# A gated mix of linear attention and a spatial MLP: w_phi laid out block-diagonally by eight small loads in place of TensorE, with the bias row, the attention weights and wo loaded in other pieces

## The chip, the cores and the metric

The kernel runs on one core of a Trainium2 chip. The metric is the device time of one execution in microseconds. Before the change the median of five runs is 208.5 us (208.04 to 208.77). One execution was also profiled; all durations and starts below are from it, in microseconds from the first instruction.

The engines are named as in the profile: PE is TensorE (PEld its weight loads), DVE is VectorE, ACT is ScalarE, POOL is GpSimd, SP is SyncE. SPq and ACTq are the instruction rows of SyncE and ScalarE, from which loads and transposes are issued.

## The reference

The input x has 2048 rows of 512. Three things are computed and mixed:

```
g  = sigmoid(sum(x * gate_w))                       # one value for each row
A: q, k, v = x @ wqkv, 32 heads of 16
   pq = q @ w_phi[h], pk = k @ w_phi[h]             # one 16x16 matrix for each head
   phi = concat(softmax(p), softmax(-p))            # 32 features, for q and for k
   kv = phi_k^T v ; z = sum over s of phi_k
   a  = (phi_q @ kv / (phi_q . z + 1e-6)) @ wo
B: z = gelu(x @ w_in) ; z1, z2 = halves of 688      # z2 is layer-normalized
   gg = w_sp @ z2 + b_sp                            # mixes the 2048 rows
   b  = (z1 * gg) @ w_out
out = g * a + (1 - g) * b
```

## The kernel before

The rows are worked on in 16 tiles of 128 (NT = 16). All is bf16, with sums in fp32.

**First stage, to about 45 us.** For each tile TensorE multiplies x (held transposed in xT) by the two halves of w_in (z_one, L195); ScalarE applies gelu into z2all and z1all; VectorE takes mean and variance (L211 to L214), and z2_norm (L276) normalizes four tiles at a time. The order on TensorE and ScalarE is written out by hand (manual_schedule): in the loop over c (four tiles each), z2 tiles, then z1 tiles. The order on SyncE, VectorE and GpSimd is made by the compiler, which plans with its own costs.

Inside this stage w_phi is folded into the q and k weights, so that pq and pk come from one product. For this w_phi must lie block-diagonally: tile wphi has 128 partitions and four blocks (kc) of 128 columns, and in block kc the eight heads 8*kc to 8*kc+7 lie as 16x16 squares on the diagonal, zero elsewhere. Before the change this layout is made in three steps. One load puts w_phi into 16 partitions of wphiE (L140). wphi_fold (L302), called after c == 1, multiplies wphiE by a 0/1 matrix eexp, which repeats the 16 rows in all eight groups of 16 partitions (four matmuls, L305), and VectorE multiplies the result by a block mask mask_bd while copying it into wphi (L310). eexp and mask_bd are made by GpSimd (L151 to L161). Then fold(qk) (L324) multiplies the transposed weights wqkT by wphi in 32x32 pieces; fold(1), for k, is done at c == 2 and fold(0), for q, at c == 3.

The bias b_sp is needed as a column for each tile. A row tile brow, of which 16 partitions are loaded by a GpSimd DMA (L118), is transposed by one matmul with the identity in b_T (L299), called after z2_tile(3), and copied to bT by VectorE (L300).

The small PSUM tiles of this stage (x transposes, gate, b_T, wphi_fold, half of a fold) take turns in two buffers, pq0 and pq1 (pq_tile).

**SyncE's queue** issues, in this order: x tiles and w_in, six transposes of x (L135, L137), w_phi (L140), the transpose of the q and k weights into wqkT in one piece (L141), the v weights wv in one load (L142), and w_sp transposed in four pieces (L147). Later it issues transposes of eq, o and ucat and, after row tile 7 of the second stage, wo and w_out into slabs of wspT that are no longer read (load_out_weights, L450 to L457).

**Second stage, from 45 us.** For each tile: k and q features (L372, L376), v (L412), the kv sums (L428), and half a tile of w_sp @ z2 (L463), whose result VectorE joins with bT and z1all into ucat (L468). Then, with kv complete, attention (L476), and the output products with wo (L500) and w_out (L502, L505), scaled and stored (L516).

The lines that the change touches are 72 to 75 (tiles), 116 to 118, 140 to 145, 151 to 164, 302 to 312, 340, 354 and 450.

Of the kernel before, what the change touches and what calls it, by code (L numbers as in the profile page):

```python
# [8 lines left out]
ALU = mybir.AluOpType  # L9
AX = mybir.AxisListType  # L10
FP32 = mybir.dt.float32
BF16 = mybir.dt.bfloat16
I32 = mybir.dt.int32

P = 128
S = 2048
D = 512
H = 32
DH = 16
# [3 lines left out]
NT = S // P  # L23
NDT = D // P
# [11 lines left out]
def kernel(  # L36
# [14 lines left out]
    nc = tc.nc  # L51
# [6 lines left out]
    early = early_cm.__enter__()  # L58
# [6 lines left out]
    wv_sb = kvw.tile([P, NDT, D], BF16, name="wv_sb")  # L65
# [3 lines left out]
    z2all = pers.tile([P, NT, FH], BF16, name="z2all")  # L69
    z1all = pers.tile([P, NT, FH], BF16, name="z1all")  # L70
    wqkT = early.tile([P, 8, D], BF16, name="wqkT")
    wphiE = early.tile([P, H, DH], BF16, name="wphiE")
    eexp = early.tile([P, P], BF16, name="eexp")
    wphi = early.tile([P, NDT, P], BF16, name="wphi")
    mask_bd = early.tile([P, P], BF16, name="mask_bd")
    mask64 = pers.tile([P, NG, DH], BF16, name="mask64")
    mask4 = pers.tile([P, NG], BF16, name="mask4")
    kvz = pers.tile([P, 8, AW], BF16, name="kvz")
# [17 lines left out]
    brow = early.tile([P, P], BF16, name="brow")  # L96
# [10 lines left out]
        out=ramp[:, 0, :], data0=ones32[:, :], data1=zeros[:, :], initial=0.0,  # L107
# [4 lines left out]
    for q in range(4):  # L112
        qs = slice(32 * q, 32 * q + 32)
        nc.vector.tensor_tensor(
            out=ident[qs, qs], in0=ramp[qs, 0, :], in1=ramp[qs, 1, :], op=ALU.is_equal)
    nc.gpsimd.memset(brow[:], 0.0)
    nc.gpsimd.memset(wphiE[:], 0.0)
    nc.gpsimd.dma_start(out=brow[0:NT, :], in_=B_b_sp.rearrange("(t p) -> t p", p=P))  # L118
    def load_z2w(eng, dt):
        eng.dma_start(out=w_z2[:, dt, 0:FH], in_=w_in_v[:, dt, FH:F])  # L120

# [8 lines left out]
        out=xs[:, 2:4, :], in_=x2[2 * P:4 * P, :].rearrange("(i p) d -> p i d", p=P))  # L130
    for h in range(2):
        nc.sync.dma_start(
            out=w_z1[:, 2 * h:2 * h + 2, :], in_=w_in_v[:, 2 * h:2 * h + 2, 0:FH])
    for i in range(4, 8):
        nc.sync.dma_start_transpose(out=xT[:, :, i * P:(i + 1) * P], in_=x2[i * P:(i + 1) * P, :])  # L135
    for q in range(2, NCH):
        nc.sync.dma_start_transpose(  # L137
            out=xT[:, :, q * CH:(q + 1) * CH], in_=x2[q * CH:(q + 1) * CH, :]
        )
    nc.sync.dma_start(out=wphiE[0:DH, :, :], in_=A_w_phi.rearrange("h e f -> e h f"))  # L140
    nc.sync.dma_start_transpose(out=wqkT[:, :, :], in_=A_wqkv[:, 0:2 * D])  # L141
    nc.sync.dma_start(  # L142
        out=wv_sb[:, :, :],
        in_=A_wqkv[:, 2 * D:3 * D].rearrange("(dt p) n -> p dt n", p=P),
    )
    for q in range(NCH):
        nc.sync.dma_start_transpose(  # L147
            out=wspT[:, :, q * CH:(q + 1) * CH], in_=B_w_sp[q * CH:(q + 1) * CH, :]
        )
    nc.gpsimd.memset(mhalf[:], -0.5)  # L150
    nc.gpsimd.memset(eexp[:], 0.0)  # L151
    nc.gpsimd.affine_select(
        out=eexp[:, :], in_=eexp[:, :], pattern=[[0, 8], [-1, 16]],
        compare_op=ALU.not_equal, fill=1.0, base=0, channel_multiplier=1,
    )
    nc.gpsimd.memset(mask_bd[:], 1.0)
    nc.gpsimd.affine_select(
        out=mask_bd[:], in_=mask_bd[:], pattern=[[-16, 8], [0, 16]],
        compare_op=ALU.is_ge, fill=0.0, base=0, channel_multiplier=1,
    )  # L160
    nc.gpsimd.affine_select(  # L161
        out=mask_bd[:], in_=mask_bd[:], pattern=[[16, 8], [0, 16]],
        compare_op=ALU.is_ge, fill=0.0, base=15, channel_multiplier=-1,
    )
    nc.gpsimd.memset(mask4[:], 1.0)
    nc.gpsimd.affine_select(
        out=mask4[:], in_=mask4[:], pattern=[[-32, NG]],
        compare_op=ALU.is_ge, fill=0.0, base=0, channel_multiplier=1,
    )
    nc.gpsimd.affine_select(  # L170
        out=mask4[:], in_=mask4[:], pattern=[[32, NG]],
        compare_op=ALU.is_ge, fill=0.0, base=31, channel_multiplier=-1,
    )
    nc.gpsimd.tensor_copy(
        out=mask64[:, :, :], in_=mask4[:, :, None].to_broadcast([P, NG, DH]))
# [7 lines left out]
    def next_turn(kind, n):  # L183
        turn[kind] += 1
        return f"{kind}{(turn[kind] - 1) % n}"
# [4 lines left out]
    def pq_tile(shape, dtype=FP32):  # L190
        return psF.tile(shape, dtype, name="pq", tag=next_turn("pq", 2))
# [24 lines left out]
    def z2_tile(tt):  # L216
        z2_out(tt, z_mm(tt, w_z2, FH + 1))
# [44 lines left out]
    def z1_tile(tt):  # L262
        zp = z_mm(tt, w_z1, FH)
        nc.scalar.activation(  # L264
            out=z1all[:, tt, :].rearrange("p (j n) -> p j n", j=2), in_=zp[:, :, 0:HF],
            func=AF.Gelu_apprx_tanh,
        )

    def z2_norm(ts):
        sl = slice(ts[0], ts[-1] + 1)  # L270
        nc.gpsimd.tensor_scalar(
            out=veps[:, sl], in0=mv[:, sl, 1], scalar1=1e-5, scalar2=None, op0=ALU.add
        )
        nc.gpsimd.tensor_tensor(out=rstd[:, sl], in0=veps[:, sl], in1=mhalf[:, sl], op=ALU.pow)
        for tt in ts:
            nc.vector.tensor_scalar(  # L276
                out=z2all[:, tt, :], in0=z2all[:, tt, :],
                scalar1=mv[:, tt, 0:1], scalar2=rstd[:, tt:tt + 1],
                op0=ALU.subtract, op1=ALU.mult,
            )  # L280
# [16 lines left out]
    def b_T():  # L297
        bt = pq_tile([P, NT])
        nc.tensor.matmul(bt[:, :], lhsT=brow[:, :], rhs=ident[:, 0:NT], start=True, stop=True)  # L299
        nc.vector.tensor_copy(out=bT[:, :], in_=bt[:, :])  # L300

    def wphi_fold():  # L302
        wps = pq_tile([P, NDT, P])
        for kc in range(NDT):
            nc.tensor.matmul(  # L305
                wps[:, kc, :], lhsT=eexp[:, :],
                rhs=wphiE[:, kc * 8:(kc + 1) * 8, :].rearrange("e h f -> e (h f)"),
                start=True, stop=True,
            )
        nc.vector.tensor_tensor(  # L310
            out=wphi[:, :, :], in0=wps[:, :, :],
            in1=mask_bd[:, None, :].to_broadcast([P, NDT, P]), op=ALU.mult,
        )

    def fold(qk):
        dst = (wq_p if qk == 0 else wk_p)[:].rearrange("p dt n -> p (dt n)").rearrange(
            "p (m r f) -> p r m f", r=4, f=32)
        pair = zp_tile()
        banks = [pair[:, 0, :], pair[:, 1, :], pq_tile([P, CH])[:, :], pq_tile([P, CH])[:, :]]
        for m in range(NDT * NDT):  # L320
            dt, kc = divmod(m, NDT)
            for r in range(4):
                rows = slice(32 * r, 32 * r + 32)
                nc.tensor.matmul(  # L324
                    banks[r][:, m * 32:(m + 1) * 32],
                    lhsT=wqkT[rows, qk * 4 + kc, dt * P:(dt + 1) * P],
                    rhs=wphi[rows, kc, rows], start=True, stop=True,
                )

        def take(out, in_):  # L330
            nc.scalar.copy(out=out, in_=in_.rearrange("p (m f) -> p m f", f=32))

        nc.scalar.copy(out=dst[:, 0:2], in_=pair[:, :, :].rearrange("p r (m f) -> p r m f", f=32))
        return [lambda: take(dst[:, 2], banks[2]), lambda: take(dst[:, 3], banks[3])]

    with tc.manual_schedule(engines={mybir.EngineType.PE, mybir.EngineType.Activation}):
        z2_first_two()
        z2_tile(2)
        z2_tile(3)
        b_T()  # L340
        for c in range(NCH):
            ts = list(range(c * 4, c * 4 + 4))
            for tt in ts:
                if c > 0:
                    z2_tile(tt)
                if c >= 2 and tt % 4 == 1:
                    later = fold(3 - c)
            for tt in ts:
                z1_tile(tt)
                if c >= 2 and tt % 2 == 0:  # L350
                    later.pop(0)()
            z2_norm(ts)
            if c == 1:
                wphi_fold()

    psA_cm.__exit__(None, None, None)
    psF_cm.__exit__(None, None, None)
# [87 lines left out]
    def load_out_weights():  # L445
        slabs = wspT[:, :, 0:D]
        w_main = [slabs[:, 0:5, :], slabs[:, 5:10, :]]
        w_rem, wo_t = slabs[:, 10, :], slabs[:, 11:11 + NDT, :]
        nc.gpsimd.memset(w_rem, 0.0)
        nc.sync.dma_start(out=wo_t, in_=A_wo.rearrange("(g p) n -> p g n", p=P))  # L450
        for i in range(2):
            nc.sync.dma_start(
                out=w_main[i],
                in_=B_w_out[i * REM:i * REM + 5 * P, :].rearrange("(ft p) n -> p ft n", p=P),
            )
        nc.sync.dma_start(out=w_rem[0:REM, :], in_=B_w_out[5 * P:FH, :])
        nc.sync.dma_start(out=w_rem[P - REM:P, :], in_=B_w_out[0:REM, :])  # L457
        return w_main, w_rem, wo_t
# [95 lines left out]
    with tc.manual_schedule(engines={mybir.EngineType.PE, mybir.EngineType.Activation}):  # L554
# [3 lines left out]
        for tt in range(NT):  # L558
# [7 lines left out]
            if tt == 7:  # L566
                w_main, w_rem, wo_t = load_out_weights()
# [51 lines left out]
```

The softmax here doesn't subtract the row's maximum and nothing guards it: scores larger than these inputs give would overflow.

## Time and profile before

| what | value |
|---|---|
| median of five runs | 208.5 us (208.04 to 208.77) |
| the profiled execution | 208.5 us |
| its span, first to last instruction | 206.8 us |
| granted TensorE clock | 0.999 |
| TensorE busy | 202.8 us, 98% of the span |
| VectorE / ScalarE / GpSimd busy | 129.0 / 77.0 / 46.5 us |
| L305, expansion of w_phi, TensorE | 4 matmuls of 128 columns |
| L310, mask multiply, VectorE | 0.69 us |
| L299, bias transpose, TensorE | 1 matmul of 16 columns |
| L140, w_phi load | 1.49 us to issue, 4.5 us to landing |
| L141, wqkT transpose | 4.57 us to issue, 6.7 us to landing |
| L118, bias load on GpSimd | 0.75 us to issue, 4.2 us to landing |

The page has six parts: busy time by engine; the span in 40 equal slices with the busy share in tenths; the transfer queues; the chain of work that ended last, which is followed back from the last instruction to what released each step; the costliest groups of instructions; and the issues of loads with their time to landing. A row of the timeline has the start, the length, the engine, the line, the operation, what it writes and reads, and how many like instructions are merged in it. For a load issue (SPq, ACTq) the length is that of the issue alone; the data land later. Matmuls of one row overlap in their last part, so their cost is read from the distance between starts, or from the chain.

### The profile page before, as it was taken

Reading aid. Unit: us, or ns where it says so; the run is one execution under the profiler, and the core shown is the slowest. Engines: PE = TensorE matmul, PEld = TensorE weight load, DVE = VectorE, ACT = ScalarE, POOL = GpSimd, SP = SyncE. Lnnn points to the kernel's source line nnn. Section 1 sums busy time; section 2 is a strip of 40 time slices with the busy share of each in tenths; the row PEclk is TensorE's granted clock in tenths of the full one; section 3 lists DMA queues with packets and bytes.
Section 4 is the critical chain, followed back from the end, with each engine's and each line's share of the span. In section 5 each row is a group of like instructions: output and inputs, shape, how many; then the busy total and the mean of one; then the engine's idle time right before and its main releaser. Section 6 shows DMA issues by size and latency. Waiting matters only on the chain.

```text
span 206.8 us, 3967 instructions
## 1 busy us (share of the span) xinstructions
PE 202.8 (98%) x1552; PEld 121.2 (59%) x1552; DVE 129.0 (62%) x278; ACT 77.0 (37%) x124; POOL 46.5 (22%) x78
## 2 busy tenths in 40 slices
PE   8999999999999999999999999999999999999994
PEld 4666666665666555556565666555455555665642
DVE  2477766656977776979797778555466553633330
ACT  3666668786322233333323032222261126002322
POOL 7020202020532327244242422222204220200000
PEclk9999999999999999999999999999999999999999
DMA  5999999999932025950413226756656467653442
GB/s 179 270 158 235 251 290 212 239 272 258 219 78 40 3 38 114 344 81 19 89 34 58 51 41 125 141 108 62 116 150 85 83 112 181 62 104 68 128 89 78
DMA packets 88971, 27.22 MB, mean 132 GB/s; under 512 B 82968, under 2 KB 88952, under 8 KB 88952
## 3 DMA queue, kind: packets, MB, share of 16 engines
q1 hardware_dynamic: 86176, 24.37, 60.5%
q10 hardware_dynamic: 2744, 2.60, 3.8%
q8 instruction: 12, 0.20, 0.4%
q14 instruction: 7, 0.06, 0.1%
q0 software_dynamic: 32, 0.00, 0.0%
HBM read 4.41 MB, written 2.10 MB: 31 GB/s over the span
## 4 chain that ended last, share of the span: by engine, by line
PE 96%; DMA 2%; SPq 0%; DVE 0%; issue 0%
PE mm L463 36%; PE zp L195 18%; PE mm L372 14%; PE mm L502 8%; PE mm L500 7%; PE mm L412 7%; DMA w_z<-in_B_w_in_dram 2%; PE at L476 2%; PE kvacc L428 2%; PE mm L505 1%; PE zp L324 0%; PE pq L284 0%; SPq L124 0%; SPq L122 0%; PE pq L324 0%; DVE ob L512 0%
## 5 line engine op out<-in xcount | busy, mean ns | idle before, releaser
L463 PE MATMUL mm<-z2all,wspT 128*128 128x344 bf16 x512 | 79.9, 309 | 0.0
L463 PEld LDWEIGHTS <-wspT 128*128 128x128 bf16 x512 | 49.0, 98 | 25.7 <-issue 0.4
L195 PE MATMUL zp<-w_z,xT 128*128 128x344 bf16 (+1 forms) x256 | 39.1, 310 | 0.1
L376 ACT ACTIVATE eq<-mm 128x512 bf16<-128x512 f32 x32 | 17.4, 594 | 51.3 <-POOL eq L389 21.5
L380 DVE TENSOR_REDUCE zs<-eq 128x64 f32<-128x1024 bf16 x16 | 19.5, 1220 | 20.3 <-ACT eq L376 20.3
L195 PEld LDWEIGHTS <-xT 128*128 128x128 bf16 x256 | 24.6, 98 | 12.0 <-issue 0.2
L468 DVE SCALAR_TENSOR_TENSOR ucat<-mm,bT,z1all 128x344 bf16<-128x344 f32 x32 | 17.4, 544 | 21.9 <-PE mm L463 21.9
L389 POOL TENSOR_TENSOR eq<-eq,ratio 128x512 bf16<-128x512 bf16 x16 | 16.9, 1056 | 50.2 <-DVE ratio L388 41.7
L376 ACT ACTIVATE ek<-mm 128x512 bf16<-128x512 f32 x32 | 17.3, 600 | 27.2 <-PE mm L372 27.2
L516 ACT ACTIVATE ob<-mm,g_inv 128x512 bf16<-128x512 f32 (+1 forms) x16 | 10.9, 681 | 32.8 <-PE mm L505 28.3
L380 DVE TENSOR_REDUCE zs<-ek 128x64 f32<-128x1024 bf16 x16 | 19.3, 1209 | 2.8 <-ACT ek L376 2.8
L502 PE MATMUL mm<-wspT,uT 128*128 128x512 bf16 (+2 forms) x85 | 20.1, 366 | 0.0
L372 PEld LDWEIGHTS <-xT 128*128 128x128 bf16 x128 | 12.2, 98 | 13.0 <-PE mm L505 0.8
L389 POOL TENSOR_TENSOR ek<-ek,ratio 128x512 bf16<-128x512 bf16 x16 | 16.9, 1057 | 2.0 <-DVE ratio L388 1.2
L500 PE MATMUL mm<-wspT,oT 128*128 128x512 bf16 (+2 forms) x68 | 16.6, 366 | 0.0
L372 PE MATMUL mm<-wq_p,xT 128*128 128x512 bf16 x64 | 16.4, 379 | 0.0
L412 PE MATMUL mm<-wv_sb,xT 128*128 128x512 bf16 x64 | 16.4, 379 | 0.0
L372 PE MATMUL mm<-wk_p,xT 128*128 128x512 bf16 x64 | 16.4, 379 | 0.0
L213 DVE BATCH_NORM_STATS2 bn<-z2all 128x6 f32<-128x344 bf16 x32 | 14.9, 502 | 0.0
L210 ACT ACTIVATE z2all<-zp 128x688 bf16<-128x688 f32 x16 | 11.8, 744 | 6.7 <-PE zp L195 6.3
L264 ACT ACTIVATE z1all<-zp 128x688 bf16<-128x688 f32 x16 | 11.9, 744 | 5.1 <-PE zp L195 5.1
L502 PEld LDWEIGHTS <-uT 128*128 128x128 bf16 x85 | 8.2, 98 | 9.2
(80 smaller groups left out, 147.5 us busy)
## 6 DMA issues: line engine op xcount, KB each, us to landing
out_dram<-ob ACTq DMA_DIRECT2D x15, 128.0 KB, 1.8
wspT<-in_B_w_out_dram SPq DMA_DIRECT2D x2, 640.0 KB, 4.9
w_z<-in_B_w_in_dram SPq DMA_DIRECT2D x2, 344.0 KB, 4.8
w_z<-in_B_w_in_dram ACTq DMA_DIRECT2D x3, 172.0 KB, 3.5
wv_sb<-in_A_wqkv_dram SPq DMA_DIRECT2D x1, 512.0 KB, 4.5
wspT<-in_A_wo_dram SPq DMA_DIRECT2D x1, 512.0 KB, 4.7
xs<-in_A_x_dram SPq DMA_DIRECT2D x2, 128.0 KB, 3.1
xs<-in_A_x_dram SPq DMA_DIRECT2D x1, 256.0 KB, 5.0
```

Source lines behind the costliest of these rows:

```text
L195: nc.tensor.matmul(zp[:, j, 0:n], lhsT=xT[:, dt, tt * P:(tt + 1) * P], rhs=wt[:, dt, j * HF:j * HF + n], start=(dt == 0), stop=(dt == NDT ...
L213: nc.vector.bn_stats(out=bn6[:, tt, j, :], in_=z2v[:, j, :])
L264: nc.scalar.activation(out=z1all[:, tt, :].rearrange("p (j n) -> p j n", j=2), in_=zp[:, :, 0:HF], func=AF.Gelu_apprx_tanh,)
L372: nc.tensor.matmul(ps[:, :], lhsT=xT[:, dt, tt * P:(tt + 1) * P], rhs=w[:, dt, :], start=(dt == 0), stop=(dt == NDT - 1))
L376: nc.scalar.activation(out=e[:, :, a, :], in_=ps[:, :].rearrange("p (h f) -> p h f", f=DH), func=AF.Exp, scale=1.0 - 2.0 * a)
L380: nc.vector.tensor_reduce(out=z[:].rearrange("p h a -> p (h a)"), in_=e[:].rearrange("p h a f -> p (h a) f"), axis=AX.X, op=ALU.add,)
L389: nc.gpsimd.tensor_tensor(out=e[:, :, 1, :], in0=e[:, :, 1, :], in1=ratio[:, :, None].to_broadcast([P, H, DH]), op=ALU.mult)
L412: nc.tensor.matmul(v_ps[:, :], lhsT=xT[:, dt, tt * P:(tt + 1) * P], rhs=wv_sb[:, dt, :], start=(dt == 0), stop=(dt == NDT - 1))
L463: nc.tensor.matmul(gp[:, 0:HF], lhsT=wspT[:, st, tt * P:(tt + 1) * P], rhs=z2all[:, st, j * HF:(j + 1) * HF], start=(st == 0), stop=(st == ...
L468: nc.vector.scalar_tensor_tensor(out=ucat[tt % NU][:, c0 + j * HF:c0 + (j + 1) * HF], in0=gp[:, 0:HF], scalar=bT[:, tt:tt + 1], in1=z1all[ ...
L500: nc.tensor.matmul(acc, lhsT=oT[:, g, :], rhs=wo_t[:, g, c0:c1], start=(g == 0), stop=False)
L502: nc.tensor.matmul(acc, lhsT=uT[:, i + ft, :], rhs=w_main[i][:, ft, c0:c1], start=False, stop=False)
```

## The change

The layout of wphi is made by loads: GpSimd clears wphi, and eight SyncE loads, one for each position u in the group of eight heads, put the 16x16 squares of heads u, u+8, u+16 and u+24 into 16 partitions of wphi. wphiE, eexp, mask_bd, wphi_fold and its mask multiply are gone. The bias row is loaded by SyncE, after the transposes of x, and b_T is called where wphi_fold was. The transpose into wqkT is in two pieces, the k weights first; the v weights and wo are loaded in two pieces each.

```diff
-    wphiE = early.tile([P, H, DH], BF16, name="wphiE")
-    eexp = early.tile([P, P], BF16, name="eexp")
     wphi = early.tile([P, NDT, P], BF16, name="wphi")
-    mask_bd = early.tile([P, P], BF16, name="mask_bd")
...
     nc.gpsimd.memset(brow[:], 0.0)
-    nc.gpsimd.memset(wphiE[:], 0.0)
-    nc.gpsimd.dma_start(out=brow[0:NT, :], in_=B_b_sp.rearrange("(t p) -> t p", p=P))
+    nc.gpsimd.memset(wphi[:], 0.0)
...
-    nc.sync.dma_start(out=wphiE[0:DH, :, :], in_=A_w_phi.rearrange("h e f -> e h f"))
-    nc.sync.dma_start_transpose(out=wqkT[:, :, :], in_=A_wqkv[:, 0:2 * D])
-    nc.sync.dma_start(
-        out=wv_sb[:, :, :],
-        in_=A_wqkv[:, 2 * D:3 * D].rearrange("(dt p) n -> p dt n", p=P),
-    )
+    nc.sync.dma_start(out=brow[0:NT, :], in_=B_b_sp.rearrange("(t p) -> t p", p=P))
+    for qk in (1, 0):
+        nc.sync.dma_start_transpose(
+            out=wqkT[:, qk * NDT:(qk + 1) * NDT, :], in_=A_wqkv[:, qk * D:(qk + 1) * D])
+    heads = A_w_phi.rearrange("(kc u) e f -> u e kc f", u=8)
+    for u in range(8):
+        us = slice(u * DH, (u + 1) * DH)
+        nc.sync.dma_start(out=wphi[us, :, us], in_=heads[u])
+    for h in range(2):
+        nc.sync.dma_start(
+            out=wv_sb[:, 2 * h:2 * h + 2, :],
+            in_=A_wqkv[h * 2 * P:(h + 1) * 2 * P, 2 * D:3 * D].rearrange("(dt p) n -> p dt n", p=P),
+        )
...
-    nc.gpsimd.memset(eexp[:], 0.0)
-    nc.gpsimd.affine_select(
...
-    nc.gpsimd.memset(mask_bd[:], 1.0)
-    nc.gpsimd.affine_select(
...
-    def wphi_fold():
...
         z2_tile(2)
         z2_tile(3)
-        b_T()
...
             if c == 1:
-                wphi_fold()
+                b_T()
...
-        nc.sync.dma_start(out=wo_t, in_=A_wo.rearrange("(g p) n -> p g n", p=P))
+        for h in range(2):
+            gs = slice(2 * h, 2 * h + 2)
+            nc.sync.dma_start(
+                out=wo_t[:, gs, :],
+                in_=A_wo[h * 2 * P:(h + 1) * 2 * P, :].rearrange("(g p) n -> p g n", p=P))
```

More of the change, by code (lines that the diff above doesn't have):

```diff
@@ L150 @@
     nc.gpsimd.memset(mhalf[:], -0.5)
-    nc.gpsimd.memset(eexp[:], 0.0)
-    nc.gpsimd.affine_select(
-        out=eexp[:, :], in_=eexp[:, :], pattern=[[0, 8], [-1, 16]],
-        compare_op=ALU.not_equal, fill=1.0, base=0, channel_multiplier=1,
-    )
-    nc.gpsimd.memset(mask_bd[:], 1.0)
-    nc.gpsimd.affine_select(
[L158 to L164, printed above, removed]
     nc.gpsimd.memset(mask4[:], 1.0)
@@ L300, in b_T @@
         nc.vector.tensor_copy(out=bT[:, :], in_=bt[:, :])
-    def wphi_fold():
[L303 to L313, printed above, removed]
     def fold(qk):
```

## The prediction

> **What bounds the kernel now.** I read the page's busy shares and slices first, then the chain of work that ended last, then that chain in order of time over the first 30 us.
>
> ```profile
> span 206.8 us, 3967 instructions
> PE 202.8 (98%) x1552; PEld 121.2 (59%) x1552; DVE 129.0 (62%) x278; ACT 77.0 (37%) x124; POOL 46.5 (22%) x78
> PE   8999999999999999999999999999999999999994
> PEclk9999999999999999999999999999999999999999
> DMA  5999999999932025950413226756656467653442
> PE 96%; DMA 2%; SPq 0%; DVE 0%; issue 0%
> ```
>
> TensorE is busy in every slice at full clock and is 96% of the chain. So a microsecond counts only if it is taken off TensorE's own row of instructions, or if TensorE is made to wait. The DMA line shows the second thing that matters: the transfers are saturated from 5 to 57 us (ten nines, slices of 5.2 us), and all the moved loads but that of wo lie in there.
>
> ```profile
> 1.74 4.48 DMA w_z<-in_B_w_in_dram
> 6.22 0.04 issue
> 6.26 1.33 PE zp L195 x8
> ...
> 8.62 2.34 PE zp L195 x16
> 10.96 0.01 PE pq L299
> 10.97 14.03 PE zp L195 x96
> 25.00 0.22 PE pq L305 x4
> 25.23 2.34 PE zp L195 x16
> 27.57 0.12 PE zp L324 x2
> ```
>
> Columns: start, length, what. From 6.26 us the chain is TensorE without a gap. The w_phi expansion (L305) stands in it with 0.22 us, the bias transpose (L299) with 0.01 us. 96 matmuls take 14.03 us, so 146 ns each.
>
> **The change, part by part.**
>
> *Expansion removed.* Four matmuls (L305) at 0.22 us in the chain go: **-0.22 us**. The VectorE mask multiply (L310, 0.69 us at 25.35) goes too, but VectorE then idles 1.17 us before its next work at 27.21: nothing. On GpSimd the bias DMA (0.75), eexp (0.23 + 0.37) and mask_bd (0.23 + 0.36 + 0.35) go, 2.29 us; all lie before 4.6 us, and GpSimd's next work, at 13.38, follows 8.79 us of idle: nothing. The memset of wphi replaces one of the same size (0.53 us).
>
> *Bias transpose moved* from 10.80 to where the expansion was. The chain's 0.01 us leaves one place and comes in at the other: zero (0.03 at most, from the starts of the neighbouring matmuls). Its VectorE copy (0.16) comes after the four normalizations that end at 25.44, into the gap before 27.21. It takes the expansion's place in the ring of two pq buffers and frees it at about 25.6, before the fold at 27.3. The row must be there by 24.8: issued at 14.1, it lands by 18.6 even at the 4.5 us that the w_phi load needed in that place.
>
> *Software queue emptied.* Over the first 10 us its 32 packets take 0.3% of the 16 transfer engines, 0.03 us of each. The chain there is the L120 load that ends at 6.22: between 0 and -0.2 us, the second being TensorE's gap before 6.26. I take **-0.03 us**, the row's own share.
>
> *The SyncE queue, 14 to 24 us.* This is the part that could cost something.
>
> ```profile
> 4.03 0.89 SPq L132 DMA_DIRECT2D w_z<-in_B_w_in_dram  x2
> 4.97 5.20 SPq L135 DMA_TRANSPOSE xT<-in_A_x_dram  x4
> 10.22 3.77 SPq L137 DMA_TRANSPOSE xT<-in_A_x_dram  x2
> 14.11 1.49 SPq L140 DMA_DIRECT2D wphiE<-in_A_w_phi_dram  x1
> 15.64 4.57 SPq L141 DMA_TRANSPOSE wqkT<-in_A_wqkv_dram  x1
> 20.26 0.58 SPq L142 DMA_DIRECT2D wv_sb<-in_A_wqkv_dram  x1
> 20.89 33.97 SPq L147 DMA_TRANSPOSE wspT<-in_B_w_sp_dram  x4
> ```
>
> New order: bias row from 14.11 (0.42, as the L122 to L129 loads take 0.41 to 0.44), two wqkT halves of 4.57 / 2 = 2.29 each, so the eight w_phi loads start at about 19.2. Each writes 16 partitions, 64 runs of 32 bytes. No row has this form. The bounds of one issue are 0.37 (the smallest SyncE load, L450 or the last store) and 1.49 (the whole w_phi load, 512 such runs). I take 0.47, an ordinary issue with its gap; an eighth of the runs stands nearer to it. Eight make 3.8, so the last would issue at about 22.5.
>
> One wait may come in. L132 at 4.03 is the ninth load issue of the program on the SyncE and ScalarE queues; it goes to a fresh tile and still waits 1.4 us, until the first load (0.81 + 3.1) has landed. I read this as eight completion semaphores used in turn. Counting on, the bias row is the 17th issue, the wqkT halves are 18 and 19, the w_phi loads 20 to 27. So the last w_phi load waits for the second half of wqkT. Undivided, wqkT landed 15.64 + 6.7 = 22.3. The transfers show 290 GB/s while it moves and about 1.5 us at 113 to 185 GB/s for w_phi's runs ahead of it (17.0 to 18.5). These 1.5 us move behind it, while between two parts of w_sp there is a dip of about 1 us, which the split may add: 21.8. That is before 22.5 and binds nothing. Landing takes 1.5 us (last store) to 4.5 (the old w_phi load, behind a transpose): I take 2.5, so w_phi is complete at 22.5 + 2.5 = **25.0**, and 27.0 at the longest. The fold needs it at 27.49 - 0.22 = **27.27**. Cost zero, cover 0.3 to 3.3 us.
>
> The partition-disjoint pair L456 and L457 (83.76 and 84.47, landing in 4.9) shows that such loads into one tile don't wait for each other.
>
> Behind it in the queue: the two wv loads, then w_sp, at about 23.9 in place of 20.89, 3.0 later. wv is read first at 47.0 and would land by about 28.4. The first part of w_sp, 12.0 to landing, comes at about 36 and is read first at 47.7: 11.7 us of cover, and the second part is read only at 84.0. The first uT transpose (56.29) goes 1 to 2 us later, and is read at 129.9. wo in two loads adds one issue of 0.37 to 0.57 at 81 us, ahead of uT, w_out and eqT transposes; wo is read at 129.0, the eqT at 117 and later. All nothing.
>
> *A rule against the change.* The rows: three loads issue at 0.81, 1.27 and 1.74 on SyncE and land 3.1 to 4.5 later, so latencies overlap. The Trainium skill, "DMA: Bandwidth & Descriptors", Rules for kernel authors, says to coalesce many small transfers, as one under 64 KB is mostly overhead, and its section on the anatomy of one DMA gives about 2.0 us of fixed cost. An estimate by that page with the eight one after the other is 16 us, complete at 35 and a stall of 8 us: 216. The rows speak against such a serial sum.
>
> **Sum.** The profiled execution took 208.5 us, 1.7 more than its span, and equals the median of the five runs (208.04 to 208.77). 208.5 - 0.22 - 0.03 = 208.25, span 206.55. That is 0.12%, less than the 0.2% (0.42 us) that a measurement of this kernel can tell from no change.
>
> **The rivals.**
>
> *More than the matmuls goes (faster).* For it: the bias load is the only use of the software queue, and 1.7 us lie outside the span, which the trace doesn't resolve; the start is bound by a load. Against it: its 32 packets are 0.3%. With the 0.2 us before 6.26 and another 0.15 of the 1.7 us: 208.5 - 0.22 - 0.2 - 0.15 = 207.9; bounds 207.5 and 208.08.
>
> *w_phi comes late (slower).* TensorE works in order, so the fold at L324 holds everything. It decides when the last load issues after 27.27 - 2.5 = 24.8, that is from (24.8 - 19.2) / 8 = 0.70 us an issue on. For it: one old issue took 1.49. At that price the last issue ends at 19.2 + 11.9 = 31.1 and lands by 32.6: a stall of 5.3, 213.6. Against it: all other plain issues lie at 0.34 to 0.66, and the old one went out just behind two transposes. A mild case, 1 us of stall, gives 209.25.
>
> *Another order on VectorE (slower).* The two first zs reductions (48.5 to 50.9) run before the first reciprocal, not in program order, so the order is the compiler's plan, which other load times may change; VectorE is full from 51 to 56. If TensorE then waits for one bank twice for a VectorE operation of 0.56 us: +1.1 - 0.25, 209.35. Against it: in the chain no VectorE wait stands in that stage now.
>
> *It doesn't do what it says.* The gain is eaten by new small waits of the fold: 208.45, within the bound.
>
> **How the numbers follow.** Forecast 208.25: 0.45. Gain eaten, 208.45: 0.07. Faster, 207.9: 0.28. w_phi late: 0.12 (a third of it mild). VectorE order: 0.08. Faster by over 0.2% 0.28, within 0.2% 0.52, slower by over 0.2% 0.20. The range holds the first three cases with the bounds of the start, the mild late case and the VectorE case: 207.6 to 209.4; the large stall and the farthest gain stay outside. The likeliest case's own range is 207.95 (gap at the start closed, a little noise) to 208.6.
>
> **What would show it.** Right: L305 gone and the matmul train before the fold running on to it; the fold's first weight load at about 27.2; w_phi's last load landing before 26; no wait on a load after 6.3 us. Wrong: an idle stretch of TensorE just before L324, SyncE issues of w_phi above 0.7 us, a first matmul train starting clearly before 6.2, or a difference between time and span other than 1.7.

## The result, and the profile after

The changed kernel takes 208.15 us (median of 38 runs, 207.66 to 208.99) against 208.56 us for the kernel before, timed again beside it (74 runs, 207.88 to 209.51). The ratio is **0.9985**, 95% interval 0.9978 to 0.9992: about 0.31 us gained. The profiled execution of the changed kernel took 208.56 us with a span of 206.83, so this one execution doesn't show the gain; the spread from one execution to the next is larger than the effect. That is why the span has to be taken apart.

The page after:

```profile
span 206.8 us, 3973 instructions
PE 202.5 (98%) x1548; PEld 120.9 (58%) x1548; DVE 129.2 (62%) x277; ACT 77.0 (37%) x124; POOL 44.5 (22%) x72
PE   8899999999999999999999999999999999999994
DMA  6998499999996014951413226756565667553442
PE 95%; DMA 2%; ACT 1%; SPq 0%; DVE 0%; issue 0%
```

TensorE is still the bound: 0.3 us less busy time, four matmuls less. Two things are new: a dip in the transfers in the fifth slice (20.7 to 25.9 us, where the eight small loads run), and 1% of ScalarE in the chain. The chain in order of time shows where both matter:

```profile
1.75 4.84 DMA w_z<-in_B_w_in_dram
6.59 0.04 issue
6.63 1.33 PE zp L184 x8
...
9.00 16.35 PE zp L184 x112
25.35 0.01 PE pq L288
25.36 2.36 PE zp L184 x16
...
38.34 5.96 PE zp L184 x40
44.30 0.02 issue
44.33 0.74 ACT z1all L253
45.07 0.48 ACT wq_p L307
45.55 0.04 issue
45.60 1.89 PE mm L347 x8
```

- *The expansion is gone.* 112 matmuls run in one piece up to the bias transpose (0.01 us). From the first full train to the fold's first weight load it took 27.49 - 6.26 = 21.23 us before and 27.64 - 6.63 = 21.01 now: -0.22. The two weight loads, before and then after:

```profile
27.49 0.56 PEld L324 LDWEIGHTS <-wqkT 32*128 32x128 bf16 x64 [0.29 <-issue]
```

```profile
27.64 0.56 PEld L300 LDWEIGHTS <-wqkT 32*128 32x128 bf16 x64 [0.28 <-issue]
```

- *The start* is 0.37 later in this execution, since the w_in load took 4.84 to land and not 4.48.
- *A new wait.* Before, the train after the second fold ran from 38.19 straight into the first k tile at 45.30, 7.11 us. Now the chain leaves the train at 44.30; the train itself runs on to 45.46, and the first k tile follows only at 45.60, behind ScalarE's last cast of wq_p: 7.26. Before, a first k matmul started 0.15 us after the train's last one; now it is 0.45 (45.15 to 45.60), a wait of about 0.31. As the second k tile had a small wait before too (0.13, gone now), the loss is read at the first w_sp product: 48.02 - 38.19 = 9.83 before, 48.35 - 38.34 = 10.01 now, +0.18. The chain before, and the rows of the new wait after:

```profile
38.19 7.11 PE zp L195 x48
45.30 1.86 PE mm L372 x8
47.16 0.86 PE mm L412 x4
48.02 2.04 PE mm L463 x14
```

```profile
43.25 2.21 PE L184 MATMUL zp<-w_z,xT 128*128 128x344 bf16 x14
44.97 0.58 ACT L307 CAST wq_p<-pq 128x512 bf16<-128x512 f32 x1
45.60 1.89 PE L347 MATMUL mm<-wk_p,xT 128*128 128x512 bf16 x8
```

The SyncE queue, as issued:

```profile
14.13 0.50 SPq L136 DMA_DIRECT2D brow<-in_B_b_sp_dram  x1
14.69 6.10 SPq L138 DMA_TRANSPOSE wqkT<-in_A_wqkv_dram  x2
20.88 3.91 SPq L143 DMA_DIRECT2D wphi<-in_A_w_phi_dram  x8
24.83 0.94 SPq L145 DMA_DIRECT2D wv_sb<-in_A_wqkv_dram  x2
25.81 35.89 SPq L150 DMA_TRANSPOSE wspT<-in_B_w_sp_dram  x4
```

The eight loads take 0.49 us each. The first, just behind the transposes, lands 3.0 us after its issue, the last four 1.6 to 1.7 us. The last is issued at 24.36 and lands at 25.97; the fold's first weight load is at 27.64.

The third place is the end. The last row of SyncE's queue is the last store, at 204.19 before and 204.51 after; the span ends 2.59 us later before, but 2.33 us later now. The two stores, before and then after:

```profile
204.19 0.37 SPq L514 DMA_DIRECT2D out_dram<-ob  x1
```

```profile
204.51 0.37 SPq L493 DMA_DIRECT2D out_dram<-ob  x1
```

The closing instructions (L614 before, L593 after) as the trace groups them, before and then after; columns: count, shortest/median/longest in ns, first to last start:

```profile
L614 SPq EVENT_SEMAPHORE  x8: 17/28/28, 204.6 to 206.7; - x8
L614 POOLq EVENT_SEMAPHORE_RANGE_CLEAR  x1: 139/139/139, 206.3 to 206.3; - x1
```

```profile
L593 SPq EVENT_SEMAPHORE  x7: 17/28/28, 204.9 to 206.8; - x7
L593 POOLq EVENT_SEMAPHORE_RANGE_CLEAR  x1: 98/98/98, 206.4 to 206.4; - x1
```

One closing wait of SyncE is gone with the software queue, and the clearing of the semaphores is 41 ns shorter. What the groups don't show is the order of the waits. These are the trace's records of SyncE after the last store (us from the span's start, semaphores waited for; the last store's own in brackets):

```
before: 204.61 S104 | 205.53 S105,S103 | 205.71 [S114],S100 | 205.78 S115,S106 | 205.84 S116,S102 | 205.90 S117,S118 | 205.97 S99 ... end 206.78
after:  204.92 S105,S104 | 204.99 S106,S103 | 205.05 S107,S100 | 205.85 S108,S102 | 206.02 [S109],S110 | 206.08 S99 ... end 206.83
```

SyncE waits for all completion semaphores in a fixed order, mostly two at a time, 0.062 us for each record that is already satisfied. What stands ahead of the last store's semaphore is passed while the store is still on its way. What stands behind it is paid after it has landed: three pairs before, none now (the single S99 in both).

So over the span: a start that differs from one execution to the next, -0.22 for the expansion, +0.18 for the first k tile, and -0.27 at the end (2.327 - 2.594 unrounded). Without the start that is -0.31, which is what the timed runs gave.

### The profile page after: what moved, and what is told of

It is laid out like the page before. It is cut to its first block, busy times and chain, and to the rows that moved or that the text cites. A ratio compares the mean times of both kernels' runs of the same rounds, so it can differ in the third digit from the quotient of the medians.

```text
span 206.8 us, 3973 instructions
## 1 busy us (share of the span) xinstructions
PE 202.5 (98%) x1548; PEld 120.9 (58%) x1548; DVE 129.2 (62%) x277; ACT 77.0 (37%) x124; POOL 44.5 (22%) x72
## 4 chain that ended last, share of the span: by engine, by line
PE 95%; DMA 2%; ACT 1%; SPq 0%; DVE 0%; issue 0%
PE mm L442 36%; PE zp L184 17%; PE mm L347 14%; PE mm L481 8%; PE mm L479 7%; PE mm L387 7%; DMA w_z<-in_B_w_in_dram 2%; PE at L455 2%; PE kvacc L403 2%; PE mm L484 1%; PE zp L300 0%; ACT z1all L253 0%; ACT wq_p L307 0%; PE pq L273 0%; SPq L120 0%; SPq L118 0%
```

## The experiments

The first four were set up before the closing records had been read. Each ratio is to the kernel before, timed again beside that run (11 or 12 executions of each, 4 of e8, 1 of e9). Theory **S** put the unexplained 0.27 us at the start, where the bias load on the software queue had been; **N** held that nothing but the expansion counts; **W** that the new wait of the first k tile costs 0.18, because there is one pq tile fewer and the two buffers change their turns.

**e1: the bias row alone** (on the kernel before).

```diff
-    nc.gpsimd.dma_start(out=brow[0:NT, :], ...)
+    nc.sync.dma_start(out=brow[0:NT, :], ...)      # after the transposes of x
...
-        b_T()                                      # after z2_tile(3)
...
             if c == 1:
+                b_T()
                 wphi_fold()
```

> The kernel before with one part of the change alone: the bias row loaded on SyncE after the x transposes and b_T called after c == 1, ahead of wphi_fold; the expansion on TensorE stays, and the two pq buffers keep their turns. Theory S (emptying the GpSimd queue at the start lets the first w_in loads land earlier, worth about 0.27 us, since 0.31 measured = 0.22 expansion + 0.27 start - 0.18 of a new wait of the first k tile): ratio 0.9987, and the first train of w_in matmuls starts on average earlier. Theory N (the start is unchanged, the gain is the expansion's alone): ratio 1.000 within 0.0005.

Measured: 0.9985 (0.9974 to 0.9996). A gain, but the first full train starts at 6.25, as before (6.26), and all up to 48.02 is alike. The trace differs at its end: 2.45 us from the last store to the end in place of 2.59. N (1.000 within 0.0005) keeps only the edge of the interval, and the 0.14 us of the trace speak against it; S has its gain, but not in its place.

**e2: the changed kernel with the bias row back on GpSimd.**

```diff
+    nc.gpsimd.dma_start(out=brow[0:NT, :], ...)
...
-    nc.sync.dma_start(out=brow[0:NT, :], ...)
```

> The changed kernel with the bias row back on GpSimd's queue at the start (b_T stays after c == 1). Theory S: it loses 0.27 us against the changed kernel, ratio to before 0.9998 (0.22 of the expansion gained, 0.18 lost to the wait of the first k tile). Theory N: it keeps all of the gain, 0.9985.

Measured: 0.9995 (0.9982 to 1.0008), near S's forecast, though the interval holds N's 0.9985 too. But the start, 6.40, is earlier than the changed kernel's 6.63, and the end is longer, 2.46 against 2.33. Again the end.

**e3: the changed kernel with the turns put back.**

```diff
             if c == 1:
+                turn["pq"] += 1
                 b_T()
```

> The changed kernel with one turn of the pq ring skipped ahead of b_T, so that the folds take the two buffers in the order of the kernel before. Theory W (with one pq tile fewer the first k tile of the second stage falls on the bank that the last cast of wq_p frees at 45.55, and TensorE loses about 0.18 us there): no wait before the first k tile, the stretch from the second fold's end to the first k tile back from 7.26 to 7.11, and 0.15 to 0.18 us less than the changed kernel, ratio to before 0.9977. Rival (the wait only takes the place of the one before the second k tile): the same as the changed kernel, 0.9985.

Measured: 0.9970 (0.9956 to 0.9983). The chain:

```profile
37.91 7.11 PE zp L184 x48
45.02 0.22 PE mm L348
```

The train runs into the first k tile again, 7.11 us. W holds, since the rival's 0.9985 lies outside the interval: one line that computes nothing is worth 0.18 us by the trace (first train to last store 197.70, against 197.88).

**e4: the w_phi part alone** (on the kernel before: eight loads, no wphiE, eexp, mask_bd and wphi_fold).

```diff
-    nc.sync.dma_start(out=wphiE[0:DH, :, :], ...)
     nc.sync.dma_start_transpose(out=wqkT[:, :, :], ...)
+    heads = A_w_phi.rearrange("(kc u) e f -> u e kc f", u=8)
+    for u in range(8):
+        us = slice(u * DH, (u + 1) * DH)
+        nc.sync.dma_start(out=wphi[us, :, us], in_=heads[u])
...
             if c == 1:
-                wphi_fold()
```

> The kernel before with the w_phi part alone: eight loads (after the undivided wqkT) in place of the expansion; the bias row stays on GpSimd and b_T where it was. One pq tile fewer, so the wait of the first k tile comes in. Theories S and W: -0.22 + 0.18 = -0.04 us, ratio 0.9998. Theory N: -0.22, ratio 0.9989, or 0.9985 if the expansion's gain is larger than its matmuls. w_phi complete by about 25, no wait before the fold in any of them.

Measured: 0.9997 (0.9983 to 1.0011). The interval holds every theory's figure, so the trace has to decide. By it the part that names the change gains nothing by itself: the expansion's 0.22 is eaten by the k tile's wait (7.26 again), and the end is 2.68, the longest so far. w_phi is complete at 25.0, as expected.

By now the starts showed no order: 6.26, 6.40 and 6.20 with the row on GpSimd, 6.63, 6.25 and 6.20 without. Theory **E** took S's place: the end counts, by what stands behind the last store's semaphore. It says that loads anywhere in the program matter, since semaphores are handed out in turn.

**e5: the splits alone** (on the kernel before: wqkT, wv and wo in two loads each).

```diff
-    nc.sync.dma_start_transpose(out=wqkT[:, :, :], in_=A_wqkv[:, 0:2 * D])
+    for qk in (1, 0):
+        nc.sync.dma_start_transpose(
+            out=wqkT[:, qk * NDT:(qk + 1) * NDT, :], in_=A_wqkv[:, qk * D:(qk + 1) * D])
...
```

> The kernel before with the splits alone: wqkT, wv and wo in two loads each, all else as before (three loads more). Theory E (the end counts: SyncE's closing waits go through the eight completion semaphores in a fixed order, those behind the last store's cost about 0.062 us each after it has landed; three loads more bring the last store from the fifth semaphore to the eighth): the stretch from the last store's issue to the end falls from 2.59 to about 2.40, ratio 0.9991, and the rest of the span stays. Theory S (the software queue at the start counts) and the prediction: no change, 1.000.

Measured: 0.9994 (0.9973 to 1.0015), too wide to tell 0.9991 from 1. The trace tells: 2.41 us from the last store to the end (2.40 expected), and 197.92 us from the first full train to the last store (197.93 before).

**e6: e3 with one load more** (wo in three).

```diff
-        for h in range(2):
-            gs = slice(2 * h, 2 * h + 2)
+        for g0, g1 in ((0, 2), (2, 3), (3, 4)):
...
```

> The changed kernel with the pq turn restored (as e3) and wo in three loads instead of two: one load more, hidden 40 us ahead of its use, which brings the last store from the eighth semaphore to the first. Theory E: seven semaphores are left behind it in place of none, the stretch from the last store to the end grows from 2.34 to about 2.75, ratio to before 0.9970 + 0.0020 = 0.9990. Theory S: the same as e3, 0.9970 to 0.9977.

Measured: 0.9983 (0.9968 to 0.9997); from the last store to the end 2.43, not 2.75. The expectation had the order wrong: the first semaphore in turn, S100, stands in the third pair of the closing waits and not in the first, so two pairs are left behind it, 0.09 us more than in e3, as in e1, whose last store has the same place (2.45). The mechanism stays, its order is the one of the records.

**e7: the casts taken earlier** (on the changed kernel).

```diff
-                if c >= 2 and tt % 2 == 0:
+                if c >= 2 and tt % 4 < 2:
                     later.pop(0)()
```

> The changed kernel with the two casts of each fold's pq buffers taken after the first and second z1 tile of a group instead of the first and third; the pq turns stay as changed. Theory W (the first k tile waits for the bank that the second cast of wq_p frees): the cast ends about 1.2 us earlier, the wait of 0.31 us before the first k tile goes, the stretch from the second fold's end to the first k tile is 7.1 again, ratio to before 0.9985 - 0.0008 = 0.9977 or a little lower. Rival (the wait is on another buffer of the first stage): 0.9985, the wait stays.

Measured: 0.9971 (0.9954 to 0.9988), the same as e3 by another way. The interval just holds the rival's 0.9985; the chain decides, since the wait is gone.

```profile
37.99 7.11 PE zp L184 x48
45.10 1.85 PE mm L347 x8
```

So it is the last cast of wq_p that the first k tile waited for. e3 and e7 beat the kernel before in the timed runs. That they also beat the changed kernel is shown by the traces (0.18 and 0.17 us between first train and last store); their intervals overlap with its own.

**e8: sixteen w_phi loads** (on the changed kernel).

```diff
-        nc.sync.dma_start(out=wphi[us, :, us], in_=heads[u])
+        for k in range(2):
+            ks2 = slice(2 * k, 2 * k + 2)
+            nc.sync.dma_start(out=wphi[us, ks2, us], in_=heads[u, :, ks2, :])
```

> The changed kernel with sixteen w_phi loads of half the size, eight loads more, so that the last store keeps its semaphore. The rival of the prediction that w_phi comes late, at the measured prices (0.49 us an issue, first issue 20.9, 1.65 us to landing): the last of sixteen issues at 28.2 and lands at 29.9, TensorE waits 2.2 us before the fold, ratio to before 0.9985 + 0.0106 = 1.009. If issues of half the runs are shorter, or the fold has more cover than read: less than 1.003.

Measured: 1.0116 (1.0078 to 1.0154). The fold's weight loads in the trace; the brackets give idle time and what ended it:

```profile
27.21 0.10 PEld L302 LDWEIGHTS <-wqkT 32*128 32x128 bf16 x3 [0.28 <-issue]
28.40 0.12 PEld L302 LDWEIGHTS <-wqkT 32*128 32x128 bf16 x8 [1.09 <-DMA wphi<-in_A_w_phi_dram]
28.92 0.47 PEld L302 LDWEIGHTS <-wqkT 32*128 32x128 bf16 x53 [0.41 <-DMA wphi<-in_A_w_phi_dram]
```

An issue costs no less for half the runs (7.86 / 16 = 0.49 us), and TensorE waits on the last ones. In this execution the loads begin at 19.89, an early case, and the stretch from the first train to the last store is 199.53, 1.65 us more than the changed kernel's; at a begin of 20.9, as in the changed kernel's profile, it would be 2.7, by an estimate that moves everything by the later begin. The timed runs gave 2.4 over the kernel before, so 2.7 over the changed one. This is the slow rival of the prediction, made to happen by the number of the issues and not by the price of one.

**e9: e3 with four loads more** (wv and wo in four each).

```diff
-    for h in range(2):
+    for h in range(4):
         nc.sync.dma_start(
-            out=wv_sb[:, 2 * h:2 * h + 2, :],
+            out=wv_sb[:, h:h + 1, :],
...
```

> As e3, with wv and wo in four loads each: four loads more, which bring the last store to the fourth semaphore. In the traces SyncE's closing waits come in pairs, and the pair that holds the last store's semaphore decides how many are left: after e3's, none but the last single one; after this one's, which stands in the first pair, four more pairs. Theory E with that order: 2.344 + 4 x 0.062 = 2.59 us from the last store's issue to the end, the rest as e3. If the order of the waits doesn't count: 2.34.

A single execution, at 208.43 beside 208.27 for the kernel before, so the times decide nothing. Its trace: 2.62 us from the last store to the end (2.59 expected). The rest was not as e3: the first oT transpose took 4.58 us to land, TensorE waited for it at 128.9, and the stretch before the end is 0.45 longer. What delayed this transpose stays open.

All together. The middle is from the first full train to the last store's issue, the end from there on; the sum is against 200.52 before. Pairs are those paid after the landing.

| kernel | start | middle | end (pairs) | middle + end | timed ratio, interval |
|---|---|---|---|---|---|
| before | 6.26 | 197.93 | 2.59 (3, software queue) | 0 | 1 |
| after | 6.63 | 197.88 | 2.33 (0) | -0.31 | 0.9985 (0.9978 to 0.9992) |
| e1 | 6.25 | 197.93 | 2.45 (2) | -0.14 | 0.9985 (0.9974 to 0.9996) |
| e2 | 6.40 | 197.88 | 2.46 (1, software queue) | -0.18 | 0.9995 (0.9982 to 1.0008) |
| e3 | 6.20 | 197.70 | 2.34 (0) | -0.48 | 0.9970 (0.9956 to 0.9983) |
| e4 | 6.20 | 197.89 | 2.68 (4, software queue) | +0.05 | 0.9997 (0.9983 to 1.0011) |
| e5 | 6.36 | 197.92 | 2.41 (0, software queue) | -0.19 | 0.9994 (0.9973 to 1.0015) |
| e6 | 6.63 | 197.70 | 2.43 (2) | -0.39 | 0.9983 (0.9968 to 0.9997) |
| e7 | 6.27 | 197.71 | 2.33 (0) | -0.48 | 0.9971 (0.9954 to 0.9988) |
| e8 | 6.19 | 199.53 | 2.34 (0) | +1.35 | 1.0116 (1.0078 to 1.0154) |
| e9 | 5.95 | 198.15 | 2.62 (4) | +0.25 | one execution |

A hundredth of a per cent is 0.02 us, so each sum of after and e1 to e7 lies inside its timed interval; e8's lies below, and its profiled execution, 209.78, was the fastest of its four (209.78 to 212.02). The start shows no difference by queue: 6.20 to 6.40 with the row on GpSimd, 5.95 to 6.63 without (means 6.31 of four and 6.30 of seven profiles).

## Why the prediction was right, step by step

Forecast 208.25 and 0.12% faster; measured 0.15% (0.08 to 0.22). The time and the sign held, and of the two terms of the sum the first held as worked out. Two effects that the prediction put at nothing or nearly so, +0.18 at the first k tile and -0.27 at the end, nearly cancel: that the total came out so close is to that extent luck.

- *Expansion removed, -0.22:* right to the hundredth (21.23 to 21.01), and the fold's first weight load moved as forecast once the start's 0.37 is taken off (27.64 - 0.37 = 27.27). e4 and e2 hold it too.
- *Bias transpose moved, zero:* right for TensorE (0.01) and for the VectorE copy.
- *"It takes the expansion's place in the ring of two pq buffers":* this failed. The place was the same, but the ring had one tile fewer, so each later tile fell on the other buffer, and the bank that the last cast frees became the first one that the second stage asks for: +0.18 (e3, e7).
- *Software queue emptied, -0.03 at the start:* not shown. The starts show no difference (6.31 and 6.30 on average), but they scatter by 0.7 us, which would hide 0.03. What the runs do show lies in the closing: about 0.07 (2.41 of e5 against 2.33, both with no pair left), a part of it the shorter clearing. From S99's record to the end it is 0.75 to 0.77 us in the seven kernels without the software queue, and 0.82 to 0.83 in the four with it.
- *The splits, "all nothing":* right for the queue, whose delays are covered, and missed for the end: the number of transfers decides which semaphore the last store gets. Three pairs at 0.062 us, -0.19 (e5).
- *The SyncE queue:* the eight loads began at 20.9 and not 19.2. The row of the whole wqkT, 4.57, was halved for each part, but the halves took 6.10 together here, and 4.5 (e8) to 6.8 (e6) in the eight kernels with the split, against 4.5 to 4.6 for the whole in three: between nothing and 2.3 us more. An issue at 0.49 (0.47 taken) and a landing in 1.7 (2.5 taken) made up for a part: complete at 25.97 where 25.0 was forecast and 27.0 was the bound, need at 27.64. That cover of 1.7 us was 0.6 (e9) to 2.2 (e4) in the other kernels with eight loads, so it is thin. w_sp went at 25.8 instead of 23.9, and the first uT transpose at 61.8, 5.5 us later than before and not 1 to 2, still without effect on TensorE.
- *The bound of 1.49 for one issue:* misread. In e1 the bias row stood directly behind the x transposes and took 1.33, and the same w_phi load behind it 0.37; in e5 the load took 0.51. So the 1.49 belonged to its place behind the transposes, not to its 512 runs, and the price of an issue for which the slow rival stood was not the load's own.
- *Eight completion semaphores in turn:* right. The last w_phi load uses the semaphore of the second half of wqkT, which landed at 23.69 (21.8 forecast), before the issue at 24.36.
- *The rule to coalesce small transfers* (the Trainium skill, "DMA: Bandwidth & Descriptors", Rules for kernel authors) didn't decide here: eight loads of 2 KB overlap their landings, and their price is SyncE's issue alone, as long as it is covered. e8 shows the rule's side, when the issues outlast the cover. The 2.0 us of fixed cost in the prediction's estimate stand on that page under the GpSimd path; SyncE's last four loads landed here 1.6 to 1.7 us after their issue.

The rivals: *more than the matmuls goes* was right that something does, 0.27 us, but inside the span at its end, and not, as far as the starts show, at the start. *w_phi comes late* didn't happen; its cover was 1.7 us, and e8 gives its price. *Another order on VectorE* falls: its instructions stand in the same order but for the two that the change removes and moves. *The gain is eaten* was true of the w_phi part alone (e4).

What stays open: e1's timed gain (0.08 to 0.54 us) is larger in its middle than the 0.14 that its trace explains, and the runs are too few to say whether that is more than chance.

## What to carry to other kernels

Taking one tile out of a rotating ring of buffers changes the turn of all later ones: look at which buffer is freed last and who asks for it first, and put the turn back by a dummy step before judging the edit. When effects are below half a per cent, split the span into start, middle and end and compare these in the traces, since here the start alone scatters by 0.7 us between executions. Count the small loads for their issue time and its cover, not for their bytes.

## What the runs showed that was not expected

The number of transfers in the whole program changes the kernel's end. The closing waits cost about 0.062 us for each record behind the last store's semaphore, so the number of hidden loads moves the end between 2.33 and 2.62 us without, and 2.41 and 2.68 with the software queue in use. And a w_phi load of half the runs takes SyncE as long to issue (0.49 us) as the one it is a half of.
